# Linear attention with a gated feed-forward block in float32: plain token pairs taken from the half that stays on chip, the sum of k by accumulating transfers, and two results kept in PSUM

## The chip, the cores and the metric

The kernel runs on one core of a Trainium2 chip. The metric is the time of one execution in device microseconds; lower is better. PE is TensorE (PEld its weight loads), DVE is VectorE, ACT is ScalarE, POOL is GpSimd, and SP is SyncE, which issues nearly all transfers.

## The reference

With x of 2048 tokens by 512, everything in float32:

```
xn  = layernorm(x)
q, k, v = split(xn @ wqkv)                    # 32 heads of 16
phi(t) = where(t > 0, t + 1, exp(t)) + 1e-6
kv  = sum over tokens of phi(k)^T v           # per head
z   = sum over tokens of phi(k)
s   = (phi(q) @ kv) / (phi(q) . z + 1e-6) @ wo
g   = silu((gelu(xn @ w_gate) * (xn @ w_up)) @ w_down)     # w_gate, w_up: 512 x 1792
out = x + s * g
```

## The kernel before

**Products.** A float32 operand is split into a high part, a copy in a reduced type made by ACT, and a low part, the difference, made by DVE. A product is three matmuls (high-high, high-low, low-high; `sum3`, line 531 of the profile). Large products go by a seven-product scheme for blocks of two by two: seven products instead of eight, with sums of blocks (S1 to S4 of weights, T1 to T4 of tokens, the "forms") made ahead and results put together behind (X, Y, Z banks; c11, c12, c21, c22).

**Tokens.** The 16 blocks of 128 tokens are taken in eight pairs (`PAIRED`), one block from each group of four, so that a pair gives two rows of blocks. Each block is loaded (x), normalised on DVE with a power on POOL in the middle (`ln`: statistics, mv, ve, rstd on POOL, xn), and transposed (pairs 0 to 4 on PE into a PSUM bank pt, pairs 5 to 7 by DVE and transfers, `turned_in`). ACT copies pt to xt. `split_x` makes the high and low slots 0 to 2 of the transposed block, `forms` the slots 3 to 6 out of T1 to T4.

**The first two pairs** (`CL = 2`) are *plain*: their k and q are made with all eight products (`plain`: 12 matmuls for each block and each of k and q, in two halves), so that work can start before the sums of the weights are ready. Their forms are needed in the feed-forward block alone. Pairs 2 to 7 use the seven products (`first_products`, `rest`). For each block, phi of k goes to SBUF (kp, `phi` and `k_out`), is added to zacc on POOL, split to pks, and multiplied with xn into four banks (`gacc`, gps in the profile). phi of q (qp) is stored to memory by SP. kp and qp share three SBUF buffers, used in turn. wk1, wk2, wq1 and wq2 are the quarters of the weights, kq and a their split forms.

**The halves.** The slots of eight token blocks fit in SBUF at a time (`XT`, four places j). Pairs 0 to 3 are the first half, tokens 0 to 1023; `spill_x` stores their slots (xh_d, xl_d). Pairs 4 to 7 overwrite them and stay. The feed-forward block then runs over the second half, loads the first half's slots again, and runs over it in the opposite order of units. `queries`, `kv_part` and `m_part` run beside it; the products S with the result of attention and the output end the program.

**Order.** Every operation is recorded with a cost and an engine. `Plan.order` lays them on the engines in a list schedule whose priorities are the numbers of the table `PRIORITY`. The order of each engine's instructions is fixed by it; an engine runs its own in that order and waits where a result is missing. The fills and warm-up matmuls (`warm`, `filler`) are matmuls of ones, with no result used, that stand where PE would be idle.

Of the kernel before, what the change touches and what calls it, by code (L numbers as in the profile page):

```python
# [9 lines left out]
F32 = mybir.dt.float32  # L10
# [8 lines left out]
WARM = 11  # L19
WARM2 = 2  # L20
CL, TURN = 2, 5
PAIRED = [(8 * (n // 4) + n % 4, 8 * (n // 4) + 4 + n % 4) for n in range(8)]
# [1455 lines left out]
```

## Time and profile before

| | |
|---|---|
| median of 3 runs | 594.05 us (593.21 to 594.99) |
| the profiled execution | 595.51 us, span 593.7 us |
| PE busy | 583.8 us, 2602 matmul records |
| DVE, ACT, POOL busy | 486.3, 322.6, 358.7 us |
| granted clock of PE | 0.999 |
| transfers | 148.37 MB, 250 GB/s on average |

A row of the timeline gives the start, the time, the engine, the line, the operation and what it writes and reads (buffer numbers left out), then how many are merged (x8) and, in brackets, the idle time before it and what ended that. In a row of groups the total busy time and the mean of one in ns stand behind the bar, then the idle time before them. A matmul record shows the whole passage through the array, so records that follow each other overlap; the distance of their starts is what a matmul takes. The k and q projections fill about the first 135 us, the two feed-forward passes nearly all of the rest.

### The profile page before, as it was taken

The page shows a single profiled execution, that of the slowest core. Times are in us where ns is not written, and L with a number is a line of the kernel's source. Part 1 is how long each engine was busy: PE and PEld are TensorE (multiplying, and loading weights), DVE is VectorE, ACT ScalarE, POOL GpSimd, SP SyncE. Part 2 cuts the span into 40 slices and gives each one's busy share as a digit, 9 for nine tenths or more (in the row PEclk, how much of TensorE's full clock was granted, in tenths as well). Part 3 has the DMA queues.
Part 4 walks back from the last instruction along what each step waited for, and adds up shares of the span by engine and source line. Part 5 has one row for each costly group of instructions (what it writes and reads, how often), then busy time and mean ns, then how long its engine had stood idle before and what let it go on. Part 6 is the DMA issues. An engine that isn't in the chain of part 4 may idle for free.

```text
span 593.7 us, 8103 instructions
## 1 busy us (share of the span) xinstructions
PE 583.8 (98%) x2602; PEld 480.2 (81%) x2602; DVE 486.3 (82%) x719; ACT 322.6 (54%) x588; POOL 358.7 (60%) x301
## 2 busy tenths in 40 slices
PE   8999999999999999999999999999999999999995
PEld 8888878887888888888888878888788888887884
DVE  6989999784898987988998975677457887779996
ACT  6867768866676654575454225534325530456841
POOL 4735475425896966877678425266334562656886
PEclk9999999999999999999999999999999999999999
DMA  8378644546958756974659999779759986899536
GB/s 288 111 230 292 192 110 125 142 160 231 353 202 283 245 211 213 335 266 160 213 189 374 354 324 343 232 277 298 266 201 323 409 288 217 272 339 361 183 116 266
DMA packets 80969, 148.37 MB, mean 250 GB/s; under 512 B 18592, under 2 KB 34208, under 8 KB 80928
## 3 DMA queue, kind: packets, MB, share of 16 engines
q1 hardware_dynamic: 80928, 147.87, 72.1%
q8 instruction: 20, 0.33, 0.2%
q14 instruction: 21, 0.17, 0.1%
HBM read 83.62 MB, written 64.23 MB: 249 GB/s over the span
## 4 chain that ended last, share of the span: by engine, by line
PE 84%; DMA 6%; DVE 5%; ACT 1%; POOL 1%; issue 1%; SPq 1%; DVEq 0%; ACTq 0%; POOLq 0%
PE FX L531 24%; PE FZ L531 12%; PE DX L531 12%; PE FY L531 6%; PE DZ L531 5%; PE gps L531 5%; PE X L531 4%; PE SX L531 3%; PE DY L531 3%; PE k L531 2%; PE q L531 2%; PE Z L531 2%; PE SZ L531 2%; DMA w<-w_d 1%; DMA pn_d<-wide 1%; DMA wide<-g_d 1%
## 5 line engine op out<-in xcount | busy, mean ns | idle before, releaser
L531 PE MATMUL FX<-Xh,w 128*128 128x512 f32 x448 | 152.3, 390 | 0.8 <-DMA w<-w_d 0.6
L1078 POOL TENSOR_TENSOR h<-h,g 128x512 f32<-128x512 f32 x42 | 63.7, 1520 | 74.8 <-DVE h L515 72.6
L531 PEld LDWEIGHTS FX<-Xh,w 128*128 128x128 f32 x448 | 83.9, 188 | 19.4 <-ACT g L1070 1.0
L515 POOL TENSOR_TENSOR h<-h,h 128x512 f32<-128x512 f32 x56 | 83.2, 1486 | 18.8 <-DVE hf3l L515 6.7
L531 PE MATMUL FX<-Xl,w 128*128 128x512 f32 x224 | 87.3, 390 | 0.0
L531 PE MATMUL FZ<-Xh,w 128*128 128x512 f32 x224 | 77.7, 389 | 0.0
L509 ACT COPY fu<-FX 128x512 f32<-128x512 f32 x56 | 32.9, 587 | 58.3 <-PE FX L531 39.7
L531 PE MATMUL gps<-pks,xns 128*128 128x512 f32 x192 | 51.1, 391 | 0.0
L531 PEld LDWEIGHTS FZ<-Xh,w 128*128 128x128 f32 x224 | 42.1, 188 | 8.7
L531 PEld LDWEIGHTS FX<-Xl,w 128*128 128x128 f32 x224 | 42.1, 188 | 8.7
L515 POOL TENSOR_TENSOR wide<-wide 128x256 f32<-128x256 f32 (+1 forms) x38 | 38.9, 1035 | 15.2 <-DVE m L515 5.5
L800 POOL TENSOR_TENSOR zacc<-zacc,kp 128x512 f32<-128x512 f32 x16 | 25.9, 1617 | 36.7 <-DVE kp L789 36.4
L1104 DVE TENSOR_TENSOR acc<-acc,DX 128x512 f32<-128x512 f32 x48 | 32.2, 680 | 14.4 <-PE DX L531 14.1
L531 PE MATMUL FZ<-Xl,w 128*128 128x512 f32 x112 | 43.6, 389 | 0.0
L531 PEld LDWEIGHTS gps<-pks,xns 128*128 128x128 f32 x192 | 35.7, 188 | 7.5 <-DVE pks L798 0.2
L531 PE MATMUL FY<-Xh,w 128*128 128x512 f32 x112 | 39.1, 390 | 0.0
L1070 ACT ACTIVATE g<-g 128x512 f32<-128x512 f32 x42 | 26.5, 633 | 20.5 <-DVE g L515 20.4
L515 POOL TENSOR_TENSOR wide<-q,zacc 128x512 f32<-128x512 f32 x16 | 21.0, 1335 | 27.1 <-DMA q<-q_d 21.1
L509 ACT COPY fe<-FX 128x512 f32<-128x512 f32 x28 | 16.4, 586 | 31.8 <-PE FX L531 23.1
L531 PE MATMUL X<-kq,Xh 128*128 128x512 f32 x96 | 31.1, 391 | 0.0
L1104 DVE TENSOR_TENSOR acc<-acc,DZ 128x512 f32<-128x512 f32 x32 | 21.7, 682 | 8.6 <-PE DZ L531 8.5
L515 DVE TENSOR_TENSOR h<-fu,FZ 128x512 f32<-128x512 f32 x28 | 19.1, 682 | 11.1 <-ACT fu L509 4.5
(369 smaller groups left out, 1553.8 us busy)
## 6 DMA issues: line engine op xcount, KB each, us to landing
w_d<-w SPq DMA_DIRECT2D x36, 512.0 KB, 4.8
w<-w_d SPq DMA_DIRECT2D x36, 512.0 KB, 6.2
wd_d<-wd SPq DMA_DIRECT2D x21, 512.0 KB, 4.5
wd<-wd_d SPq DMA_DIRECT2D x21, 512.0 KB, 5.1
x<-in_first SPq DMA_DIRECT2D x16, 256.0 KB, 3.2
q_d<-qp SPq DMA_DIRECT2D x16, 256.0 KB, 2.2
q<-q_d SPq DMA_DIRECT2D x16, 256.0 KB, 5.2
pn_d<-wide SPq DMA_DIRECT2D x16, 256.0 KB, 5.4
```

The source lines that it names most:

```text
L509: do("ACT", act(n), lambda o, i: nc.scalar.copy(o, i), dst, src, name=name)
L515: do(eng, c, lambda o, p, q: getattr(e, f"tensor_{op}")(o, p, q), dst, a, b, name=name)
L531: nc.tensor.matmul(o, v[i], v[i + 1], start=start and part == 0 and i == 0, stop=stop and part == 1 and i == len(v) - 2, skip_group_check=on)
L800: do("POOL", pool(D), lambda o, i: nc.gpsimd.tensor_add(o, o, i), zacc, p0, name="zacc")
L1070: curved("gelu", do("ACT", curve(NC), lambda o, i: nc.scalar.activation(o, i, AF.Gelu_apprx_tanh), g, ps if e is None else g, name="gelu"))
L1078: do("POOL", pool(NC), lambda o, i: nc.gpsimd.tensor_mul(o, o, i), h, g, name="h")
L1104: do("DVE", dve(NC), lambda o, i: nc.vector.tensor_add(o, o, i), a, ps, name="acc")
```

## The change

- `SEQ` takes the pairs in another order: the two plain pairs are now the first two of the half that stays, then come the four of the half that leaves, then the last two that stay. `LOC` and `XTS` give their places; `spill_x` goes by `SEQ[n] < 4`.
- The forms of the two plain pairs are made behind those of pairs 5 and 6 (`FORMS`).
- zacc is summed by accumulating transfers, issued by POOL (`gather`), in place of 16 additions on POOL.
- c11 and c12 are written over the PSUM bank that they come from (`IN_PLACE`).
- For pairs 2, 3 and 4 (`FROM_PT`), T1, T2 and T3 are made by DVE out of the bank pt, T4 stays on POOL, and ACT copies half of the second block's pt.
- The transposes without a bank of their own use bank 2, that of Y, in place of bank 1.
- One low part of wk2 moves from POOL to DVE. The warm-up has 9 + 2 matmuls in place of 11 + 2, the fills are 3, 2 and 1 in place of 4, 5 and 2.
- The first two blocks are normalised side by side, and the table of numbers that sets the order is another one throughout.

```diff
-WARM = 11
+WARM = 9
+FORMS = {5: 0, 6: 1}
+IN_PLACE = ("c11", "c12")
+FROM_PT = (2, 3, 4)
+PT_BANK = 2
+SEQ = [4, 5, 0, 1, 2, 3, 6, 7]
-PAIRED = [(8 * (n // 4) + n % 4, 8 * (n // 4) + 4 + n % 4) for n in range(8)]
+PAIRED = [(8 * (n // 4) + n % 4, 8 * (n // 4) + 4 + n % 4) for n in SEQ]
+XTS = [3, 4, 5, 12, 13, 5, 3, 5]
+LOC = [0, 1, 2, 3, 2, 3, 2, 3]
 ...
 PRIORITY = """
-702 946 1004 2779 932 2336 513 1054 ...
 ...
+    def gather(dst, src, name):
+        op = do("POOL", 1.0, lambda o, i: nc.gpsimd.dma_start(o, i, accum_op=ALU.add), dst, src, name=name)
+        op.port, op.land = False, 2.5
 ...
-        kq_split(1, wk2, k, eng="POOL")
+        kq_split(1, wk2, k, eng="POOL" if k in (1,) else "DVE")
 ...
-        pt = early.get((n, i)) or bank(1, f"pt{t}", (P, KT, P))
+        pt = early.get((n, i)) or bank(PT_BANK, f"pt{t}", (P, KT, P))
 ...
-        copy("ACT", xts[n, i], pt, D, f"xt{n}{i}")
+        if i and n in FROM_PT:
+            copy("ACT", xts[n, i][:, 0:2], pt[:, 0:2], 2 * P, f"xt{n}{i}")
+        else:
+            copy("ACT", xts[n, i], pt, D, f"xt{n}{i}")
 ...
+    def part_of(n, i, k):
+        if n in FROM_PT and i:
+            return pts[n, 1][:, 2 * k:2 * k + 2]
+        return xts[n, i][:, 2 * k:2 * k + 2]
 ...
-        tt("POOL", "sub", s(0), b[:, 0:2], a[:, 0:2], 256, "T1")
-        tt("POOL", "sub", s(1), b[:, 2:4], s(0), 256, "T2")
-        tt("POOL", "sub", s(2), b[:, 2:4], b[:, 0:2], 256, "T3")
-        tt("POOL", "sub", s(3), a[:, 2:4], s(1), 256, "T4")
+        eng = "DVE" if n in FROM_PT else "POOL"
+        tt(eng, "sub", s(0), b[0], a[0], 256, "T1")
+        tt(eng, "sub", s(1), b[1], s(0), 256, "T2")
+        tt(eng, "sub", s(2), b[1], xts[n, 1][:, 0:2] if n in FROM_PT else b[0], 256, "T3")
+        tt("POOL", "sub", s(3), a[1], s(1), 256, "T4")
 ...
-        c = U(*places, name)
+        c = ps if name.split("_")[0] in IN_PLACE else U(*places, name)
         tt("DVE", "add", c, e, ps, D, name)
 ...
-        do("POOL", pool(D), lambda o, i: nc.gpsimd.tensor_add(o, o, i), zacc, p0, name="zacc")
+        gather(zacc, p0, "zacc")
 ...
-                filler(("T", 0, 0), 4)
-        forms(n)
+                filler(("T", 0, 0), 3)
         if n >= CL:
+            forms(n)
 ...
-                        filler(("K", 0, 0, 0), 5)
-                        filler(("T", 0, 1), 2)
+                        filler(("K", 0, 0, 0), 2)
+                        filler(("T", 0, 1), 1)
 ...
-        if n < 4:
+        if SEQ[n] < 4:
             spill_x(n)
+        if n in FORMS:
+            forms(FORMS[n])
```

The order moves at the very start. On PE, before, from the warm-up to the end of the first block's k projection (pt are transposes, k_267 the projection, kq the weights, Xh and Xl the parts of the tokens, b those of the second block):

```order
L553 MATMUL warm<-ones 128x128 x11
L553 MATMUL warm_232<-ones 128x128 x2
L729 MATMUL pt_241<-ident,xn_230 128x128 x4
L553 MATMUL fill_248<-ones 128x128 x4
L531 MATMUL k_267<-kq_225,Xh_259 128x512 x3
L531 MATMUL k_267<-kq_225,Xl_265 128x512
L531 MATMUL k_267<-kq_225,Xh_259 128x512
L531 MATMUL k_267<-kq_225,Xl_265 128x512
L531 MATMUL k_267<-kq_225,Xh_259 128x512 x2
L553 MATMUL fill_293<-ones 128x128 x3
```

and now, where k_272 is the first block's projection and k_295 the second's:

```order
L596 MATMUL warm_186<-ones 128x128 x2
L596 MATMUL warm<-ones 128x128 x9
L781 MATMUL pt_249<-ident,xn_240 128x128 x4
L781 MATMUL pt_256<-ident,xn_242 128x128 x4
L596 MATMUL fill_264<-ones 128x128 x2
L574 MATMUL k_272<-kq_234,Xh_262 128x512 x2
L596 MATMUL fill_264<-ones 128x128
L574 MATMUL k_272<-kq_234,Xh_262 128x512
L574 MATMUL k_272<-kq_234,Xl_277 128x512
L574 MATMUL k_272<-kq_234,Xh_262 128x512
L574 MATMUL k_272<-kq_234,Xl_277 128x512
L574 MATMUL k_295<-kq_234,b_0_283 128x512 x2
```

The second block's transpose now stands ahead of the first projection, and products of the second block stand between the halves of the first.

On DVE, now, the piece that ends with the low part Xl_361 of the second block, which the second k projection waits for (ahead of it stand the first two xn, two kq, two statistics and two Xl):

```order
L718 BN_AGGR mv_299<-st_291 128x2
L718 BN_AGGR mv_299<-st_267 128x2
L720 TENSOR_SCALAR ve_304<-mv_299 128x2
L554 TENSOR_TENSOR kq_234<-wide,kq_234 128x512
L554 TENSOR_TENSOR b_0_283<-pt_256,b_0_283 128x256
L735 TENSOR_SCALAR xn_325<-x_209,mv_299,rstd_314 128x512
L735 TENSOR_SCALAR xn_329<-x_216,mv_299,rstd_314 128x512
L554 TENSOR_TENSOR a_337<-wide,a_306 128x512
L554 TENSOR_TENSOR kq_327<-wq_223,kq_319 128x512
L554 TENSOR_TENSOR xns_289<-xn_242,xns_289 128x512
L554 TENSOR_TENSOR Xl_361<-pt_256,Xh_293 128x256
```

A kq that POOL made, the a and kq of the q weights, and the xn of the second pair now stand ahead of that Xl.

On POOL, before, the first additions to zacc among the forms T of the plain pairs:

```order
L515 TENSOR_TENSOR T_335<-xt_253,T_335 128x256
L800 TENSOR_TENSOR zacc<-zacc,kp_367 128x512
L515 TENSOR_TENSOR T_335<-xt_253,T_335 128x256
L515 TENSOR_TENSOR T_402<-xt_371 128x256
L800 TENSOR_TENSOR zacc<-zacc,kp_408 128x512
L679 TENSOR_TENSOR rstd_444<-ve_435,neg_half 128x2
```

and now, the first of the accumulating transfers, up to the first T4 of pair 2:

```order
L722 TENSOR_TENSOR rstd_314<-ve_304,neg_half 128x2
L557 DMA zacc<-kp_385 128x512
L557 DMA zacc<-kp_398 128x512
L722 TENSOR_TENSOR rstd_471<-ve_466,neg_half 128x2
L557 DMA zacc<-kp_423 128x512
L557 DMA zacc<-kp_495 128x512
L722 TENSOR_TENSOR rstd_573<-ve_567,neg_half 128x2
L554 TENSOR_TENSOR T_638<-xt_600,T_638 128x256
```

The forms of the plain pairs are gone from here, and each transfer but the first waits on POOL for the landing of the one ahead of it.

More of the change, by code (lines that the diff above doesn't have):

```diff
@@ L18 @@
 EPS = 1e-6
-WARM = 11
+WARM = 9
 WARM2 = 2
 CL, TURN = 2, 5
-PAIRED = [(8 * (n // 4) + n % 4, 8 * (n // 4) + 4 + n % 4) for n in range(8)]
+FORMS = {5: 0, 6: 1}
+ON_ACT = ()
+IN_PLACE = ("c11", "c12")
[5 more added lines that the diff above has]
+LOC = [0, 1, 2, 3, 2, 3, 2, 3]
 XS = [t for pair in PAIRED for t in pair]
@@ L223, in do @@
         op.kb = kb / self.RATE + gap if kb else 0.0
+        if not kb:
+            op.land = 0.0
         op.port = eng == "POOL" or eng == "DVE" and cost > 0.25 and not any(v.psum for v in views)
@@ L260, in hop @@
     def hop(self, p, s):
+        if p.eng == "POOL" and p.land:
+            return p.land
         if p.eng == "SP":
@@ L553, in warm @@
             nc.tensor.matmul(o, w, w, start=True, stop=True)
-    do("PE", 4.7, warm, bank(0, "warm", (P, P)), ones, key="warm")
+    do("PE", 3.84, warm, bank(0, "warm", (P, P)), ones, key="warm")
     do("PE", 0.43 * WARM2, lambda o, w: warm(o, w, WARM2), bank(7, "warm2", (P, P)), ones, key="warm2")
@@ L680, in ln @@
            rstd, ve, neg_half)
+        by_act = XS.index(ts[0]) // 2 in ON_ACT
+        if by_act:
+            shift = little("sh", f"shift{ts[0]}", [P, n])
+            do("DVE", 0.075, lambda o, m, r: nc.vector.scalar_tensor_tensor(o, m, -1.0, r, op0=ALU.mult, op1=ALU.mult),
+               shift, mv[:, :, 0], rstd, name="shift").port = True
         for i, t in enumerate(ts):
             xns[t] = U("xn", range(4, 9), f"xn{t}")
+            if by_act:
+                do("ACT", curve(D), lambda o, i, r, b: nc.scalar.activation(o, i, AF.Identity, bias=b, scale=r),
+                   xns[t], xs.pop(t), rstd[:, i:i + 1], shift[:, i:i + 1], name=f"xn{t}")
+                continue
             do("DVE", 0.456, lambda o, i, m, r: nc.vector.tensor_scalar(o, i, m, r, op0=ALU.subtract, op1=ALU.mult),
@@ L686 @@
     xts, Ts, pts = {}, {}, {}
-    early = {(0, 1): bank(4, "pt4", (P, KT, P)), (1, 0): bank(5, "pt1", (P, KT, P)), (1, 1): bank(6, "pt5", (P, KT, P))}
+    early = {(0, 1): bank(4, "pt4", (P, KT, P)), **{(1, i): bank(5 + i, f"pt1{i}", (P, KT, P)) for i in range(2) if CL > 1}}
     def filler(after, n):
@@ L718, in transp @@
         if i == 0:
-            xts[n] = D2(3 + n % 3, f"xt{n}").map(lambda ap: ap.rearrange("p a (k c) -> p a k c", c=P))
+            xts[n] = D2(XTS[n], f"xt{n}").map(lambda ap: ap.rearrange("p a (k c) -> p a k c", c=P))
         v = xts[n]
@@ L730, in transp @@
         do("PE", 0.52, run, pt, xns[t], ident, key=("T", n, i), name="T")
-        copy("ACT", xts[n, i], pt, D, f"xt{n}{i}")
+        if i and n in FROM_PT:
+            copy("ACT", xts[n, i][:, 0:2], pt[:, 0:2], 2 * P, f"xt{n}{i}")
+        else:
+            copy("ACT", xts[n, i], pt, D, f"xt{n}{i}")
         pts[n, i] = pt
+    def part_of(n, i, k):
+        if n in FROM_PT and i:
+            return pts[n, 1][:, 2 * k:2 * k + 2]
+        return xts[n, i][:, 2 * k:2 * k + 2]
     def forms(n):
-        a, b = xts[n, 0], xts[n, 1]
+        a, b = [[part_of(n, i, k) for k in range(2)] for i in range(2)]
         T = Ts[n] = D2(ring("T", [1, 2]), f"T{n}").map(lambda ap: ap.rearrange("p a (s k c) -> p (a s) k c", s=2, c=P))
@@ L746, in forms @@
                 lambda ap: ap.rearrange("p s k c -> p (s k) c"))
-            split(xblock("h", 3 + 2 * i, 5 + 2 * i, n % 4), xblock("l", 3 + 2 * i, 5 + 2 * i, n % 4), by_slot(src), D, f"XT{i}")
+            split(xblock("h", 3 + 2 * i, 5 + 2 * i, LOC[n]), xblock("l", 3 + 2 * i, 5 + 2 * i, LOC[n]), by_slot(src), D, f"XT{i}")
     def split_x(n, i):
@@ L753, in split_x @@
         elif i == 0:
-            split(xblock("h", 0, 2, n % 4), xblock("l", 0, 2, n % 4), by_slot(pts.get((n, 0), xts[n, 0])), D, "Xa")
+            split(xblock("h", 0, 2, LOC[n]), xblock("l", 0, 2, LOC[n]), by_slot(pts.get((n, 0), xts[n, 0])), D, "Xa")
         else:
-            split(xblock("h", 2, 3, n % 4), xblock("l", 2, 3, n % 4), by_slot(pts.get((n, 1), xts[n, 1])[:, 2:4]), 2 * P, "Xb")
+            split(xblock("h", 2, 3, LOC[n]), xblock("l", 2, 3, LOC[n]), by_slot(pts.get((n, 1), xts[n, 1])[:, 2:4]), 2 * P, "Xb")
     def prod(ps, n, i, start):
         ws, xsl = PRODUCTS[i]
-        xv = [xslot(hl, xsl, n % 4) for hl in "hl"]
+        xv = [xslot(hl, xsl, LOC[n]) for hl in "hl"]
         sum3(("A", n, i), ps, [((xv[0][:, k], xv[1][:, k]), (kq(ws, 0, k), kq(ws, 1, k))) for k in range(2)],
@@ L822, in spill_x @@
         for hl in "hl":
-            a, b = [xblock(hl, *XCUT[i], n).map(lambda ap: ap.bitcast(F32)) for i in range(2)]
-            do("SP", 0.475, move_both, x_d[hl](n, (slice(None), slice(None), n)), a, b, kb=896, kind="pieces", name="pieces")
+            a, b = [xblock(hl, *XCUT[i], LOC[n]).map(lambda ap: ap.bitcast(F32)) for i in range(2)]
+            do("SP", 0.475, move_both, x_d[hl](SEQ[n], (slice(None), slice(None), SEQ[n])), a, b, kb=896, kind="pieces", name="pieces")
     def first_products(n):
@@ L841, in plain @@
         ps = bank(ring("plain", [0, 2, 3]), f"{'q' if is_q else 'k'}{n}{i}")
-        xv = [[xslot(hl, s, n % 4) for hl in "hl"] for s in range(3)]
+        xv = [[xslot(hl, s, LOC[n]) for hl in "hl"] for s in range(3)]
         if i == 0:
```

267 rows, old and new, of the table PRIORITY are left out of this document.

## The prediction

> **What bounds the kernel now.** I read the page's busy times first, then its chain, then TensorE's own waits.
>
> ```profile
> PE 583.8 (98%) x2602; PEld 480.2 (81%) x2602; DVE 486.3 (82%) x719; ACT 322.6 (54%) x588; POOL 358.7 (60%) x301
> ...
> PE 84%; DMA 6%; DVE 5%; ACT 1%; POOL 1%; issue 1%; SPq 1%; DVEq 0%; ACTq 0%; POOLq 0%
> ```
> ```profile
> PE warm L553 <- DVE neg_half L544: 1.1, 1, 1.1
> PE k L531 <- ACT Xh L509: 0.6, 1, 0.6
> PE FX L531 <- DMA w<-w_d: 0.6, 1, 0.6
> PE DX L531 <- DVE acc L1104: 0.5, 1, 0.5
> PE pkv L1236 <- DMA wide<-g_d: 0.5, 1, 0.5
> PE FX L531 <- DVE w L515: 0.2, 1, 0.2
> PE Y L531 <- ACT Xh L509: 0.2, 1, 0.2
> ```
> PE is the bound, and its named waits come to 3.7 us in all, 1.8 of them in the feed-forward stage (0.6 + 0.5 + 0.5 + 0.2). The change takes no product away, so freeing POOL or ACT gains nothing by itself. Only three kinds of PE time can go: waits, fills, and a slow start. So the next view is the timeline of the first 25 us, the engines together and then PE alone.
>
> ```profile
> 1.12 5.41 PE L553 MATMUL warm<-ones 128*128 128x128 f32 x26 [1.12 <-DVE neg_half L544]
> 5.15 0.55 DVE L683 TENSOR_SCALAR xn<-x,mv,rstd 128x512 f32<-128x512 f32 x1 [0.68 <-POOL rstd L679]
> 5.21 1.14 ACT L509 CAST kq<-wk 128x512 fp32r<-128x512 f32 x2 [3.13 <-DMA wk<-in_first]
> 6.36 0.60 PE L729 MATMUL pt<-ident,xn 128*128 128x128 f32 x4
> 6.80 1.06 PE L553 MATMUL fill<-ones 128*128 128x128 f32 x8
> 7.30 0.57 ACT L509 COPY xt<-pt 128x512 f32<-128x512 f32 x1
> 7.77 0.64 ACT L509 CAST Xh<-pt 128x256 fp32r<-128x256 f32 x2
> 8.47 0.97 PE L531 MATMUL k<-kq,Xh 128*128 128x512 f32 x3 [0.61 <-ACT Xh L509]
> 9.91 1.31 ACT L509 CAST a<-wide 128x512 fp32r<-128x512 f32 x2 [0.97 <-DMA wide<-in_first]
> 12.46 1.38 PE L553 MATMUL fill<-ones 128*128 128x128 f32 x8
> ...
> 17.09 0.39 PE L531 MATMUL k<-kq,Xl 128*128 128x512 f32 x1
> 17.31 0.84 PE L531 MATMUL k<-kq,Xh 128*128 128x512 f32 x3
> ...
> 23.43 1.52 PE L531 MATMUL gps<-pks,xns 128*128 128x512 f32 x6
> 24.79 0.84 PE L531 MATMUL k<-kq,Xh 128*128 128x512 f32 x3
> ```
> The last two rows give the price of a product: 1.36 us for six, 0.227 each. From the first transpose (6.36) to the end of the two k projections of the first pair (17.31) PE took 10.95 us. It had 24 products (5.45) and four transposes of at most 0.44 (6.36 to 6.80) to do, 7.2 in all. So 3.7 us are fills and waits. This is the largest loss of PE time anywhere, and the change rewrites just this place.
>
> **The start, worked out.** I follow the new order with the durations of these rows of DVE:
>
> ```profile
> 5.86 1.29 DVE L515 TENSOR_TENSOR kq<-wk,kq 128x512 fp32r<-128x512 f32 x2 [0.17 <-ACT kq L509]
> 7.27 0.70 DVE L674 BATCH_NORM_STATS2 st<-x 128x6 f32<-128x512 f32 x1
> 8.45 0.42 DVE L515 TENSOR_TENSOR Xl<-pt,Xh 128x256 fp32r<-128x256 f32 x1 [0.27 <-ACT Xh L509]
> 10.37 0.24 DVE L675 BATCH_NORM_AGGREGATE mv<-st 128x2 f32<-128x6 f32 x2
> 11.04 0.68 DVE L515 TENSOR_TENSOR xns<-xn,xns 128x512 fp32r<-128x512 f32 x1
> 11.64 0.15 DVE L677 TENSOR_SCALAR ve<-mv 128x2 f32<-128x2 f32 x1
> 12.67 1.00 DVE L683 TENSOR_SCALAR xn<-x,mv,rstd 128x512 f32<-128x512 f32 x2 [0.88 <-POOL rstd L679]
> ```
> Both first tokens are now loaded ahead of wk1. One more statistics instruction (about 0.6) stands ahead of the first xn, which ends at 6.3 instead of 5.7. The warm-up is 11 instructions instead of 13. At 5.41 us for 26 passes, two to an instruction, its 22 take 4.6 and end near 5.7, so PE waits some 0.6 us for xn, but the transpose starts at 6.3 to 6.4, as before. Then ACT has the two Xh casts ahead of the xt copy: pt is ready at 7.0, the casts end at 7.7, and the first k product starts at 7.75 instead of 8.47, with the second transpose already done.
>
> What ends the stretch is DVE, which has no pause in it. From its first xn (5.7) to the Xl that closes the second k projection stand four xn (2.0), two kq (1.3), two statistics (1.4), two Xl (0.8), two mv and a ve (0.4), kq (0.7), b (0.4), a, kq and xns (2.0) and Xl (0.4): 9.4 us, so that Xl ends at 15.1. Rows that follow each other overlap a little on DVE (kq: two in 1.29, one such row alone 0.68), 0.08 a row, which takes it to 13.6 at best. Three products still need it: 14.3 to 15.8. PE's own work sets the lower end: 24 products, two transposes and four fills from 7.75 on are 14.5. ACT's queue is no later: one wk2 cast waits for the seventh load. With the third landed at 5.2 and the ninth at 9.9 (the two ACT rows with a DMA behind them), that is 0.78 apiece and 8.3; the casts end at 9.4, and the products that use them stand behind 9.5. PE reaches the point of 17.31 at 15.3, between 14.5 and 15.8: **2.0 us earlier, 1.5 to 2.8**. The five fills (ten passes) and two warm-up instructions that go are inside this figure. With the pauses that remain in the new order (the first Xl: 5.7 + 1.0 + 1.3 + 0.7 + 0.4 = 9.1; b, cast behind the wk2 casts, near 10; six fills) it agrees to 0.2.
>
> **The middle (15 to 150).** These are the groups of POOL and DVE in that stretch, and two windows:
>
> ```profile
> L800 POOL TENSOR_TENSOR zacc<-zacc,kp 128x512 f32<-128x512 f32 x16 | 25.9, 1617 | 36.7 <-DVE kp L789 36.4
> L515 POOL TENSOR_TENSOR T<-xt 128x256 f32<-128x256 f32 x14 | 15.3, 1095 | 13.3 <-ACT xt L509 9.4 <-DMA w_d<-w 3.9
> ...
> L798 DVE SCALAR_TENSOR_TENSOR pks<-kp,pks 128x512 fp32r<-128x512 f32 x16 | 14.0, 876 | 0.3
> L515 DVE TENSOR_TENSOR Xl<-T,Xh 128x512 fp32r<-128x512 f32 x16 | 13.1, 822 | 1.0 <-ACT Xh L509 1.0
> ...
> L789 DVE SCALAR_TENSOR_TENSOR kp<-c,kr 128x512 f32<-128x512 f32 x12 | 8.0, 683 | 0.5 <-issue 0.5
> ...
> 20.00:30.00 10.00, 10.00 (x45) 8.26 (x44) 9.82 (x20) 7.62 (x14) 7.13 (x6) 1.00 0.19 66
> ...
> 60.00:70.00 10.00, 10.00 (x45) 8.00 (x44) 10.00 (x17) 7.82 (x14) 6.47 (x5) 1.00 0.64 211
> ```
> DVE (third busy figure of a window, after PE and PEld) is at 9.8 to 10 of 10 us here, so its load decides whether the lead of PE lasts. Added: nine subtractions of 128x256 out of PSUM (0.42 each, 3.8) and one kq (0.7). Moved behind 100 us: four low halves of the plain pairs' forms (0.82 each, 3.3). Shortened: pks and Xl take 876 and 822 ns, where kp, of the same size, takes 683. They are longer beside POOL, and POOL loses the 25.9 us of zacc and nine of its T rows. The excess is 16 x 0.19 + 16 x 0.14 = 5.3 us, of which about half should go. The sum is 4.5 - 3.3 - 2.6 = -1.4 us for DVE: the lead is not eaten.
>
> c11 and c12 in PSUM add no instruction, but hold Y's and Z's banks until kp has read them, and the transposes now share Y's bank. The tightest place is the Y of the fourth pair: 13 products (2.95 us) stand between the transpose that fills its bank and Y. The bank needs 0.6 + 0.4 + 0.4 + four DVE rows of 0.42, partly side by side: 2.4 to 3.1. So 0 to 0.2 us there, and at most 0.5 for each of three such pairs; a gain of the 0.2 of the Y wait is as likely. I take 0, with -0.3 and +1.5.
>
> **The gathers.** No row shows an accumulating transfer. Each waits on POOL for the one before it to land, and holds its kp buffer that long; there are three such buffers, used in turn by kp and qp.
>
> ```profile
> q_d<-qp SPq DMA_DIRECT2D x16, 256.0 KB, 2.2
> ...
> g_d<-acc SPq DMA_DIRECT2D x8, 256.0 KB, 6.7
> ```
> ```profile
> L800 POOL TENSOR_TENSOR zacc<-zacc,kp x16: 1283/1620/2886, 15.9 to 134.5; 128x512 f32<-128x512 f32 x16
> ```
> The bounds of its landing time L are the first two rows: the same source and size, and the slowest move of that size. I take 3.0, near the first, as transfers take only 0.19 of the 16 engines from 20 to 30 us. The first two gathers stand back to back, and qp of the first token overwrites the second one's buffer. The kp of both lie 1.4 us apart on DVE, and 14 rows stand between the second kp and that qp: seven of whole blocks (0.68), two statistics (0.70), b and Xl (0.42), two mv and a ve, 7.4 us. So it is late by 2L - 8.8 us: nothing up to L = 4.4, and 4.6 us at L = 6.7. Behind it on DVE stand the two xn of the next transposes and the last plain kp, so PE would stop for nearly all of it. Later uses lie 9 us and more apart and wait only beyond L = 6. I take 0, with 0 and +4.6. On POOL itself the rstd behind a gather needs a ve that comes 5 us later, so it is free.
>
> "SBUF — State Buffer" of the Trainium skill (SBUF: two separate sides) speaks against this: a transfer issued by GpSimd cannot get its descriptors written while VectorE holds the shared port, and 620 ns alone became 3100 ns in its measurement. An estimate by that page adds 2.5 us to L, so 5.5, and would make the sum 2.2 us worse. The rows of pks and Xl above agree that the two engines block each other here; no row shows it for a descriptor.
>
> **The rest.** Spills of the leaving half come later on SP, and the x loads that stood behind them come earlier. FFN keeps its products; the last 59 rows of PE, and DVE's last 20, are the same, so the tail stays. The 1.8 us of waits there are at places whose DMA and DVE neighbours are slightly reordered: 0, between -1.0 and +1.0.
>
> **Sum.** -2.0 + 0 + 0 + 0 against the profiled 595.5 gives 593.5; the median shown is 1.5 lower, so I expect 594.05 - 2.0 = **592.0**.
>
> **Rivals.** (1) *The start's lead is not there*, since DVE's queue fills up with what used to stand behind it (s, kq and a splits of wq1 and wq2), and the first gps and q products wait for pks and a. For it: DVE's 9.8 of 10 us from 20 on. Against: the lows moved out. Only the 0.7 of the earlier first product stays: 593.3. (2) *The gather is slow*, from L = 4.4, and turns the sign from 2L - 8.8 = 2.0, so L = 5.4; it is slower by more than 0.3% from L = 6.3, and at g_d's 6.7 ends at 592.0 + 4.6 = 596.6. How it can come without slow transfers: zacc as an instruction took 1.28 to 2.89 us (the row behind them), so up to 1.6 of it was waiting for DVE; one such wait makes L 4.6 (592.4), two make it 6.2 (595.6). For it: the port rows, the chain of 16. Against: q_d's 2.2. (3) *The clock comes later.* The warm passes take 0.208 each, the fills behind them 1.06 / 8 = 0.13, so PE is about 1.6 times slower at first. The shorter warm-up and the gap behind it could leave the first projection in that state: 12 x 0.227 x 0.6 = 1.6 more, half of it inside the waits at 9.1 and 10, so 592.8. Against: the switch lies inside 5.4 us of the old warm-up. "TensorE: Matmul & The Clock Gate" of the Trainium skill (Part 1) says that full speed is granted after a busy window of about 3.4 us that does not start with the kernel. By that rule it can fall behind the gap; the trace agrees as far as the one switch goes. (4) *POOL's relief reaches PE*: with 35 us of POOL rows gone, pks and Xl shrink to 683 throughout, the Y wait goes, the weight forms of the first units (POOL, then DVE) come earlier, and FFN's waits fall by 1.0 to 1.3: 592.0 - 1.5 = 590.5. Against: two of the three larger FFN waits are on DMA.
>
> **How the numbers follow.** My forecast 0.44, (4) 0.12, (1) 0.15, (3) 0.07, (2) 0.22. A measurement of this kernel tells about 0.3% (1.8 us) from no change, so faster is below 592.3. The forecast itself falls on that edge: with its bounds three fifths of it are faster (0.26), with all of (4) and 0.05 from the better ends of (1) and (3). Of (2) 0.07 ends about level (the one or two waits for DVE), and 0.05 of slower comes from banks and FFN at their worst together. That gives faster 0.43, same 0.37, slower 0.20. The range reaches from (4) with the start's best to L near 6.4: 589.8 to 596.0; the likeliest case alone spans 591.2 to 592.5.
>
> **What would show it.** Right: first k product near 7.8, the sixth k group (now 17.31) near 15.3, PE dense from there, gathers landing within 4.4 us, and qp of the first token with no wait on a transfer. Wrong: DVE rows qp or kp waiting on zacc's transfer (2); pt or Y waiting on DVE kp (banks); products 0.36 apart after 6.3 (3); or the lead there at 17 us and gone at 60 (1).

## The result, and the profile after

The changed kernel takes 601.84 us (median of 6 runs, 598.87 to 604.70) against 594.15 us before (6 runs): ratio 1.0128, 95% interval 1.0093 to 1.0163. It is slower by 7.7 us, where 592.0 was forecast and the range ended at 596.0. The profiled execution, the slowest of the six, took 604.7 us with a span of 602.8; before it was 595.5 and 593.7. So the two profiles lie 9.1 us apart, and it is this difference that the rows explain.

Busy times and the chain, from the page of the changed kernel:

```profile
PE 586.0 (97%) x2588; PEld 478.2 (79%) x2588; DVE 484.5 (80%) x729; ACT 322.3 (53%) x588; POOL 333.9 (55%) x291
...
PE 82%; DMA 6%; DVE 6%; ACT 2%; issue 1%; SPq 1%; POOL 1%; DVEq 0%; POOLq 0%
```

DVE lost 1.8 us, near the 1.4 forecast; POOL lost 24.8, less than the 35 of the prediction, since the 16 issues themselves take 14.4. PE is still the bound, so look at its waits (time in all, times, longest):

```profile
PE gps L574 <- ACT pks L858: 1.9, 1, 1.9
PE FX L574 <- DMA w<-w_d: 1.6, 1, 1.6
PE gps L574 <- DVE pks L859: 1.5, 3, 0.7
PE pt L781 <- DVE xn L735: 1.2, 1, 1.2
...
PE q L574 <- DVE qp L850: 1.0, 1, 1.0
PE FY L574 <- DVE g L554: 0.9, 1, 0.9
PE pt L781 <- DVE kp L850: 0.6, 1, 0.6
```

With the warm-up's 1.1, as before, and three small ones (0.4, 0.3, 0.2) these are 10.7 us; before they were 3.7. The 7.0 more are most of the 9.1. A further 1.7 is no wait at all. It shows in two windows of the changed kernel around the longest stall (third to last figure: the granted clock of PE):

```profile
110.00:112.40 2.40, 0.52 (x3) 0.10 (x1) 1.39 (x3) 0.80 (x3) 1.59 (x3) 1.00 0.81 196
112.40:116.60 4.20, 4.18 (x11) 3.32 (x12) 3.46 (x7) 3.15 (x6) 0.62 (x1) 0.59 0.79 201
```

After PE had stood still for 1.9 us the clock was at 0.59 on average for 4.2 us: eleven records of product there, where 18 fit at 0.227, so 1.7 us are lost. (By the trace it is 1.00 up to 113.2 and then 0.50 for 3.4 us.)

Where does the time go along the program? The next table is worked out from both traces: at places of the product stream with the same work still to do, it gives how much later PE is than in the kernel before (us; places by the time before).

```
place, us              20    30    60    80   100   110   160   300   end
changed kernel       -0.9   0.5   0.5   2.4   3.1   7.1   7.9   7.7   9.2
```

The start is 0.9 ahead; all of that and 7.9 us more are lost between 20 and 160, that is in the projections, and nearly half of it at one place, 100 to 110 (112 to 117 in the changed kernel's own time).

**The transfers.** Issues of the changed kernel (size each, median us from issue to landing), and what DVE and POOL wait for:

```profile
zacc<-kp POOLq DMA_DIRECT2D x16, 256.0 KB, 3.9
q_d<-qp SPq DMA_DIRECT2D x16, 256.0 KB, 2.6
```
```profile
DVE qp L850 <- DMA zacc<-kp: 4.1, 2, 2.1
DVE kp L850 <- DMA zacc<-kp: 1.1, 1, 1.1
```
```profile
POOL zacc L557 <- DMA zacc<-kp: 11.4, 4, 4.7
```

A landing takes 3.3 to 5.5 us by the trace, 3.9 in the middle, so the 3.0 of the prediction was low but its threshold of 4.4 looked safe. Still DVE stands three times. The first is the qp that the prediction named, on DVE and, for the two transfers ahead of it, on POOL:

```profile
27.65 0.69 DVE L850 SCALAR_TENSOR_TENSOR qp<-q,qr 128x512 f32<-128x512 f32 x1 [2.03 <-DMA zacc<-kp]
```
```profile
18.19 1.05 POOL L557 DMA_DIRECT2D zacc<-kp  x1 [6.01 <-DVE kp L850]
24.23 0.87 POOL L557 DMA_DIRECT2D zacc<-kp  x1 [5.00 <-DVE mv L718]
```

The first transfer lands at 23.69, the second is issued 0.54 later and lands at 27.55; then DVE goes on. (The row names DVE's mv, which ended at 24.0. With four buffers, below, the landing alone ends this wait, and the step is 0.55.) Why did the first take 5.5 us? These are the DMA queues (packets, MB, share of the 16 engines) from 18 to 21.9 us, then from 21.9 to 24:

```profile
q0 software_dynamic: 135, 0.25, 36.4%
q8 instruction: 1, 0.02, 2.1%
```
```profile
q0 software_dynamic: 9, 0.02, 5.5%
```

At 21.3 us 135 of its 144 packets are through, on fifteen of the 16 engines. The last nine run from 22.0 to 23.4, one behind the other, right behind the one packet of q8, a load of instructions that takes 20.7 to 22.0. (That the two share an engine is read from these times; the trace does not name it.) Without them the landing would have been near 21.6, so 3.4 us after the issue, by an estimate from the 0.27 us between last packet and landing.

The other two waits come from two transfers back to back again (issued at 100.24 and 105.78, landing at 105.38 and 110.92). The first wait is for the one landing, the second for both, now on DVE ahead of the longest stall of PE:

```profile
105.50 0.69 DVE L850 SCALAR_TENSOR_TENSOR qp<-X,qr 128x512 f32<-128x512 f32 x1 [2.10 <-DMA zacc<-kp]
...
111.01 0.69 DVE L850 SCALAR_TENSOR_TENSOR kp<-Z,kr 128x512 f32<-128x512 f32 x1 [1.06 <-DMA zacc<-kp]
```
```profile
112.42 1.88 PE L574 MATMUL gps<-pks,xns 128*128 128x512 f32 x5 [1.90 <-ACT pks L858]
```

### The profile page after: what moved, and what is told of

Read it like the earlier page. It is cut to its first block, busy times and chain, and to the rows that moved or that the text cites. A ratio compares the mean times of both kernels' runs of the same rounds, so it can differ in the third digit from the quotient of the medians.

```text
span 602.8 us, 8122 instructions
## 1 busy us (share of the span) xinstructions
PE 586.0 (97%) x2588; PEld 478.2 (79%) x2588; DVE 484.5 (80%) x729; ACT 322.3 (53%) x588; POOL 333.9 (55%) x291
## 3 DMA queue, kind: packets, MB, share of 16 engines
q1 hardware_dynamic: 80928, 147.87, 71.1%
## 4 chain that ended last, share of the span: by engine, by line
PE 82%; DMA 6%; DVE 6%; ACT 2%; issue 1%; SPq 1%; POOL 1%; DVEq 0%; POOLq 0%
PE FX L574 24%; PE DX L574 12%; PE FZ L574 12%; PE DZ L574 6%; PE FY L574 6%; PE gps L574 4%; PE X L574 3%; PE DY L574 3%; DMA zacc<-kp 2%; PE SX L574 2%; PE Z L574 2%; DMA w<-w_d 1%; PE SZ L574 1%; PE q L574 1%; PE k L574 1%
## 5 line engine op out<-in xcount | busy, mean ns | idle before, releaser
L557 POOL DMA_DIRECT2D zacc<-kp x16 | 14.4, 902 | 51.7 <-DVE kp L850 26.8
L1133 ACT ACTIVATE g<-g 128x512 f32<-128x512 f32 x42 | 26.6, 632 | 18.8 <-DVE g L554 18.7
L554 POOL TENSOR_TENSOR wide<-q,zacc 128x512 f32<-128x512 f32 x16 | 20.8, 1323 | 21.2 <-DMA q<-q_d 12.1
L554 DVE TENSOR_TENSOR g<-fu,FZ 128x512 f32<-128x512 f32 x28 | 19.1, 682 | 15.0 <-PE FZ L574 8.2
L548 ACT COPY fe<-FX 128x512 f32<-128x512 f32 x28 | 16.4, 587 | 27.1 <-PE FX L574 19.7
```

Source lines behind the costliest of these rows:

```text
L548: do("ACT", act(n), lambda o, i: nc.scalar.copy(o, i), dst, src, name=name)
L554: do(eng, c, lambda o, p, q: getattr(e, f"tensor_{op}")(o, p, q), dst, a, b, name=name)
L557: op = do("POOL", 1.0, lambda o, i: nc.gpsimd.dma_start(o, i, accum_op=ALU.add), dst, src, name=name)
L1133: curved("gelu", do("ACT", curve(NC), lambda o, i: nc.scalar.activation(o, i, AF.Gelu_apprx_tanh), g, ps if e is None else g, name="gelu"))
```

## The experiments

Theory A: the transfers hold the three buffers of kp and qp, because each waits for the landing of the one before and then for its own, and DVE stands for the buffer. Rivals: B, the PSUM banks that c11, c12 and the T sums now hold; C, the new order of the feed-forward stage. Those that came later (D to G) are told in the expectations. In every experiment the compute engines execute their instructions in the order of the kernel it is made from, so that only the edit and what it does to buffers differ.

### The transfers as POOL adds again

```diff
-        op = do("POOL", 1.0, lambda o, i: nc.gpsimd.dma_start(o, i, accum_op=ALU.add), dst, src, name=name)
+        op = do("POOL", 1.0, lambda o, i: nc.gpsimd.tensor_add(o, o, i), dst, src, name=name)
```

> The changed kernel with every instruction of every engine in its place; only the 16 accumulating transfers of kp into zacc are POOL adds again. Theory A (the transfer holds kp's buffer and the next transfer waits for the landing of the one before, so that DVE's next kp or qp is late): the PE gaps that end at 28.4 (1.1 us), 64.1 (0.8), 76.3 (0.8), 86.1 (0.6), 95.9 (0.6) and 112.4 (2.1 and about 1.9 of half-rate products behind it) go, 7.9 us together: 594 us, 593 to 596. Rival B (the held PSUM banks: c11 and c12 in place and three T sums read from PSUM): the gaps stay, 600 to 602. Rival C (the gaps are in what the FFN's new order does, 153 to 590): 600 to 602 too, but with the early gaps gone and the later ones grown.

Measured: 599.66 us, ratio 1.0095 (1.0080 to 1.0111). Between the theories. The wait at 112 us shrinks from 1.9 to 0.2 us and the clock stays up, but others come in its place, nearly all with DVE's own rows behind them, among them:

```profile
PE k L574 <- DVE b L554: 0.7, 1, 0.7
PE Y L574 <- DVE Xl L554: 0.6, 1, 0.6
...
PE Z L574 <- DVE c L554: 0.6, 1, 0.6
```

DVE is busy 112.9 of the 120 us from 20 to 140 here; with the transfers (four buffers, below) it is 104.8. The new order has no room for the adds, so this run undoes one cost and makes another.

### The transfers alone, in the kernel before

```diff
-        do("POOL", pool(D), lambda o, i: nc.gpsimd.tensor_add(o, o, i), zacc, p0, name="zacc")
+        do("POOL", pool(D), lambda o, i: nc.gpsimd.dma_start(o, i, accum_op=ALU.add), zacc, p0, name="zacc")
```

> The kernel before with every instruction in its place; only its 16 POOL adds of kp into zacc become accumulating transfers. Theory A: its three kp buffers are held the same way, gaps of 4 to 8 us between 17 and 140: 598 to 602 us. Rival B: nothing but the sum of k differs and POOL is relieved, so 593 to 595. Rival C: 593 to 595.

Measured: 596.12 us, ratio 1.0033 (1.0017 to 1.0050). Below A's 598, above B's and C's. DVE waits once for a transfer (kp at 136.65, 1.6 us), and PE does not stop for it. PE's one new wait behind the start, 1.0 us at 73, comes another way, over POOL:

```profile
70.64 0.86 POOL L800 DMA_DIRECT2D zacc<-kp  x1 [4.33 <-DMA zacc<-kp]
71.21 1.03 POOL L679 TENSOR_TENSOR rstd<-ve,neg_half 128x2 f32<-128x2 f32 x1
72.27 0.55 DVE L683 TENSOR_SCALAR xn<-x,mv,rstd 128x512 f32<-128x512 f32 x1 [2.32 <-POOL rstd L679]
```

POOL stands for the landing of the transfer before, its rstd comes behind that, DVE's xn waits for rstd, and qp, which PE waits for, comes behind xn. The prediction had called rstd free; in the changed kernel no wait of PE comes this way. In the old order the transfers cost 2 us (1.0 to 3.0 by the interval), of which these rows show 1.0; so the order decides how much the same 16 transfers cost.

### Four buffers, and two sums

```diff
-    def added(e, ps, name, places=("c", range(13, 16))):
+    def added(e, ps, name, places=("c", range(13, 15))):
...
-        p0 = U("p", range(18, 21), f"{nm}p{t}")
+        p0 = in_order("p", [18, 19, 20, 15], f"{nm}p{t}")
```

> The changed kernel, orders kept, with four buffers for kp and qp instead of three (the fourth is one that c11 and c12 no longer use), the transfers kept. Theory A: a phi needs the buffer of the fourth phi before it instead of the third, so most waits go: early gaps of at most 3 us instead of 7.9, 594 to 598. Rival B and C: as the changed kernel, 600 to 603.

```diff
+    def to_sum(o, i):
+        issued.append(1)
+        if len(issued) == 1:
+            nc.gpsimd.dma_start(zsum(), i)
+        else:
+            nc.gpsimd.dma_start((o, zsum())[len(issued) % 2], i, accum_op=ALU.add)
...
-        op = do("POOL", 1.0, lambda o, i: nc.gpsimd.dma_start(o, i, accum_op=ALU.add), dst, src, name=name)
+        op = do("POOL", 1.0, to_sum, dst, src, name=name)
```

> The changed kernel, orders kept, three buffers, but the transfers go in turn into two sums, which one POOL add joins behind the last (one instruction more on POOL). Theory A with the serial wait as the larger part: a transfer no longer waits for the landing before it (11.4 us of POOL's idle time in four waits), DVE's waits shrink to a single landing: 595 to 599. If one landing of 3.3 to 5.5 us by itself is what holds the buffer too long: 600 to 602. Rival B and C: 600 to 603.

Measured: 599.05 us, 1.0085 (1.0070 to 1.0100), and 599.03 us, 1.0086 (1.0071 to 1.0101). Both medians are 2.8 us below the changed kernel's (the intervals just overlap), and both miss most of what A gave them, the two sums at A's edge. With four buffers the waits at 27 and 105 us are gone, but a longer one stands where the third was, on DVE:

```profile
108.88 0.69 DVE L859 SCALAR_TENSOR_TENSOR kp<-Z,kr 128x512 f32<-128x512 f32 x1 [3.05 <-DMA zacc<-kp]
```

With two sums the waits at 27 and 111 are gone and the one at 105, for a single landing, stays (2.4 us). So each takes away one of the two ways, and the other still holds.

### Both together

The two edits above; the fourth buffer (unit 14) serves from the tenth phi on, which leaves one buffer to `added`.

> The changed kernel, orders kept, with two sums for the transfers and, from the tenth phi on, four buffers for kp and qp. Theory A (the transfers hold buffers, in two ways: the wait for the landing before, and the landing itself): DVE's waits on zacc's transfer go, and with them the PE gaps near 28 (1.1 us) and 110 to 112 (2.1, and the half-rate products behind it); against the kernel before, PE is then behind by 1 to 2.5 us at the place of 120 us (7.1 in the changed kernel, 5.0 with four buffers alone, 3.2 with two sums alone), and the time is 596 to 598. Rival D (what holds PE at 110 is the turned x that lands late, or DVE's load, and not kp's buffer): the gap stays at 1.4 us or more, 598.5 to 600.

Measured: 597.53 us, ratio 1.0052 (1.0032 to 1.0072). DVE's waits on zacc shrink from 5.2 us to 0.3, and 0.0076 of the 0.0128 is gone, 4.5 us: A's share. But the stall at 110 us does not go as A had it: 1.4 us of waiting stay, as rival D said. Its cause is now in the open, on ACT:

```profile
108.74 0.40 ACT L557 CAST Xh<-xt 128x256 fp32r<-128x256 f32 x1 [2.57 <-DMA xt<-xb_d]
109.05 0.58 ACT L557 COPY e<-X 128x512 f32<-128x512 f32 x1
109.52 0.63 ACT L876 ACTIVATE pks<-kp 128x512 fp32r<-128x512 f32 x1
```

kp is ready at 107.2, but pks stands on ACT behind the cast of a turned x (the seventh pair's second block) that has not come back from DRAM, and gps waits for pks. It was sent at 97.4 and is there at 108.7, 11.3 us; the kernel before takes 7.4 for the same block. Why? The DMA queues and issues (us to landing) of this kernel from 97 to 104 us, then of the kernel before from 86 to 97, where it turns the same pair:

```profile
q1 hardware_dynamic: 2038, 1.56, 70.4%
q0 software_dynamic: 191, 0.36, 29.9%
...
xl_d<-Xl SPq DMA_DIRECT2D x1, 640.0 KB, 4.2
xb_d<-xb SPq DMA_DIRECT2D x2, 256.0 KB, 4.1
...
xt<-xb_d SPq DMA_DIRECT2D x4, 64.0 KB, 6.3
```
```profile
q1 hardware_dynamic: 3529, 1.42, 46.4%
...
xb_d<-xb SPq DMA_DIRECT2D x2, 256.0 KB, 2.2
xt<-xb_d SPq DMA_DIRECT2D x8, 64.0 KB, 2.7
```

The way back (xt) takes 6.3 us instead of 2.7 from issue to landing. The 16 engines are full (70.4 + 29.9), where they were half idle. Two loads are new there. One is the transfers: q0 moves 0.36 MB in 29.9% of 7 us, 5.8 us of all engines for a MB, against 3.2 for q1 in the same row. The other is the spill (xl_d): before, the leaving pairs came first and were stored by 68 us; now the plain pairs are of the half that stays, the leaving pairs come third to sixth, and their stores stand among the turned x. (The slow store that the expectations below name is the next pair's; this block loses its time on the way back.)

### c11 in SBUF, and the T sums on POOL

```diff
-IN_PLACE = ("c11", "c12")
+IN_PLACE = ("c12",)
```

> Two sums, three buffers, orders kept, and c11 again in SBUF instead of in Y's bank. Theory B1 (the bank of Y, held until kp has read it, delays the transposes that share it): the gap of PE behind which pt waits for kp near 63 us (0.8 us) goes, 0.8 less than with two sums alone (599.0): 598.2, 597.5 to 598.7. Rival E (DVE's queue is late there whatever holds the bank): a gap of 0.5 us or more stays within 5 us of that place, 598.7 to 599.5.

```diff
-FROM_PT = (2, 3, 4)
+FROM_PT = ()
```

> Two sums, four buffers, orders kept, and all T sums from SBUF on POOL again: nine rows of 0.42 us leave DVE, nine of about 0.73 come to POOL. Theory E (DVE's load between 40 and 95 us is what makes pks late, gps <- DVE pks 0.8, 0.7 and 0.4 us with four buffers): these three gaps go or halve, 1 to 2 us less than with both sums and buffers: 594.5 to 596. Rival F (T on POOL comes later, and POOL's rows slow DVE's by the port): the same or more than with both, 597 to 599.

> Two sums, three buffers, c11 in SBUF and all T sums on POOL, orders kept. If B1 and E both hold: the bank gap (0.8) and half or more of the pks gaps (1 to 2) go against two sums alone (599.0): 596 to 597.3. If POOL's sums cost what they give (F): 598 to 599.

Measured for c11 in SBUF: 597.96 us, ratio 1.0059 (1.0036 to 1.0082), against 1.0086 (1.0071 to 1.0101) for two sums alone. The time lies in B1's band, but the trace reads as E: the wait of pt for kp is gone, and PE stops 0.4 us at the same place for X instead of 0.6. The profile with c11 in SBUF also started 0.7 us earlier, from the landing of the first loads, so the two times do not decide; the bank alone is worth 0.2 us at this place. The T sums on POOL, with ACT copying the whole of pt again, gain nothing: 599.15 us, 1.0076 (1.0049 to 1.0103), against 1.0052 with both, and, with c11 in SBUF too, 600.05, 1.0089 (1.0064 to 1.0114), against 1.0059. Both medians are higher and above F's bands, but the intervals overlap. E's guess on DVE's load, 594.5 to 596, falls, and the change's reading of T sums from PSUM on DVE is not what costs the time; that POOL's rows slow DVE's, as F has it, these times do not show.

### The load on the DMA engines

Three runs take theory D apart, on top of both sums and buffers, and one puts the load into the kernel before.

```diff
+    moved, held = [], []
...
     def move_both(o, a, b):
+        moved.append(1)
+        if len(moved) in (7, 8):
+            held.append((o, a, b))
+            return
...
+        if o.name == "table":
+            while held:
+                move_both(*held.pop(0))
```

> Two sums and four buffers, orders of the four compute engines kept; the four stores of the last leaving pair's forms (1.8 MB, from 79 to 103 us) are sent only behind the last pair, where their tiles hold another pair's forms, so that part of the output is of other data. Theory D (after the waits on zacc, what stops PE near 85 and 110 us is the turned x of the sixth and seventh pair: it comes late from DRAM, and ACT's pks stands behind its cast; the store takes 5.5 us there where it took 2.0 to 3.3 before, since the moved spill and the transfers, which need about 6.0 us of engine time per MB where others need 2.9, share the 16 engines): the turned x of the seventh pair lands 1 to 2 us earlier than 108.7, the gap at 110 falls from 1.5 to 1.0 us or less, 1 us less than with both (597.5): 596 to 597. Rival G (the rows of DVE that make it simply stand later in the new order): the gap stays at 1.3 or more, 597 to 598.

```diff
+        elif len(issued) in (10, 11):
+            nc.gpsimd.tensor_add(o, o, i)
```

> Two sums and four buffers, orders kept; only the tenth and eleventh transfer (issued near 98.5 and 99.1 us, landing up to 106.4) are POOL adds. Theory D: the store of the turned x takes 2 to 3.5 us instead of 5.5, the gap at 110 falls from 1.5 to 0.8 us or less, 596 to 597. Rival G: the gap stays at 1.3 or more, 597 to 598.

> Both of these together: the last leaving pair's four stores sent behind the last pair (with another pair's forms in them) and the tenth and eleventh transfer as POOL adds. Theory D: the turned x of the seventh pair lands within 7.5 us of DVE's transposing, as before (9.4 with both sums and buffers), and the gap at 110 is 0.4 us or less; 595.5 to 596.5. Rival G: a gap of 1.2 us or more stays, 597 to 598.

Measured: 595.79 us, ratio 1.0023 (1.0007 to 1.0040), without the last spill in its place; 596.79, 1.0030 (1.0016 to 1.0045), with the two adds; 596.89, 1.0036 (1.0020 to 1.0052), with both. In all three traces no gap is left at 110 us, where the five profiles with two sums so far have one of 1.3 to 1.4. The block that took 11.3 us from its store to its last load takes 9.7, 7.4 and 7.2. Either load alone can be taken away, and x comes in time: that shows the cause, and G falls. For this block the transfers are the larger of the two. The intervals of the times overlap, with each other and with both sums and buffers, so what the gap is worth is read from the traces; where adds stand in for transfers, a new gap of 0.5 to 0.6 us for DVE's Xl comes at 102 to 104 us and eats a part. What is left of PE's waits in the run without the last spill (0.4 and 0.3 not shown, and the warm-up):

```profile
PE gps L583 <- DVE pks L877: 1.0, 1, 1.0
PE FX L583 <- ACT fe L557: 0.6, 1, 0.6
PE pt L799 <- DVE kp L868: 0.6, 1, 0.6
...
PE gps L583 <- ACT pks L876: 0.3, 1, 0.3
```

The run with both lost 2 us near 80 us instead: there the turned x of the sixth pair landed 2.1 us later than in the run without the last spill, with the same instructions up to that place. Landing times in that crowd vary from run to run.

```diff
+        for n in (4, 5):
+            if o is more[n]:
+                for hl in "hl":
+                    a, b = [xblock(hl, *XCUT[i], n % 4).map(lambda ap: ap.bitcast(F32)) for i in range(2)]
+                    move_both(extra[hl, n](), a(), b())
```

> The kernel before, orders of the four compute engines kept, with one thing added: the forms of the fifth and sixth pair are also stored to DRAM (eight stores, 3.6 MB, to a place that nobody reads), so that stores stand beside the turned x as in the changed kernel. Theory D: the share of the 16 engines between 80 and 110 us rises from 0.25 to 0.55 to over 0.7, turned x lands later, and PE gets gaps of 0.5 to 2 us there: 594.7 to 596.5. Rival G: the order before leaves 3 us between landing and use, so PE keeps its time: 594 to 594.6. If it is the transfers' traffic alone that matters: as rival G.

Measured: 597.45 us, ratio 1.0046 (1.0032 to 1.0060), 2.7 us more, above D's range. The windows of this kernel (second to last figure: share of the DMA engines, 0.25 and 0.55 before in the first and last), ACT's rows and PE's waits:

```profile
80.00:90.00 10.00, 9.60 (x42) 7.62 (x41) 9.45 (x17) 6.37 (x12) 7.33 (x8) 1.00 0.86 239
...
100.00:110.00 10.00, 8.94 (x39) 6.91 (x39) 5.71 (x10) 5.87 (x12) 3.23 (x5) 1.00 0.88 262
```
```profile
99.24 0.62 ACT L509 CAST Xh<-xt 128x512 fp32r<-128x512 f32 x1 [2.17 <-DMA xt<-xb_d]
...
107.09 0.41 ACT L509 CAST Xh<-xt 128x256 fp32r<-128x256 f32 x1 [1.75 <-DMA xt<-xb_d]
```
```profile
PE X L531 <- ACT Xh L509: 2.4, 2, 1.3
```

Stores of forms beside the turned x, with no transfer on POOL at all, stop ACT and then PE in the kernel before too. That is D by itself, with one thing left open: the eight stores also stand ahead of loads on SP, and this run does not separate their issue from their load on the engines. The two adds above do: there SP's instructions are unchanged.

## Why the prediction was wrong

The places once more, as worked out above (us later than the kernel before):

```
place, us              20    30    60    80   100   110   160   300   end
changed kernel       -0.9   0.5   0.5   2.4   3.1   7.1   7.9   7.7   9.2
four buffers         -1.2  -1.2  -1.2   0.4   1.0   5.0   5.5   5.2   3.2
both                 -0.4  -0.4  -0.3   1.0   1.4   3.3   3.9   3.6   2.8
both, no last spill  -0.9  -0.9  -0.8   0.3   1.0   1.3   2.0   1.8   0.1
```

**The gathers: this term failed.** It was given 0, with rival (2) beginning at L = 4.4. The place and the mechanism of its first wait were right: DVE's qp on the second transfer. Three things in the sum were not. It used one L for both landings, where the trace has 5.5 and 3.3; their sum is 8.8, by the formula exactly no wait. It left out the steps between: 0.33 us from the end of kp to the issue, 0.54 from one landing to the next issue. And it gave DVE 8.8 us of work where qp was reached 7.8 after the first kp. Together 0.33 + 5.5 + 0.54 + 3.3 - 7.8 = 1.9, measured 2.03. At this place it was also bad luck: with 3.4 for the first landing, the estimate above without the load of instructions, the sum is -0.2, no wait. In the nine other profiles with the new order and transfers that load starts at 19.5 to 21.2 us, so it comes each time, but what it delays varies. The sentence that later uses "lie 9 us and more apart and wait only beyond L = 6" was the larger error. At 105 us DVE came back to the buffer of the first of two transfers 3.6 us after its kp (99.84 to 103.40), so one landing of 5.1 was too long. The second of two back to back holds its buffer for two landings, and at 5.1 us each that was too long at 111. All waits of this kind cost 4.5 us of the 7.7 (ratio 1.0128 to 1.0052; 2.1 to 6.9 by their intervals), with the fall of the clock behind the longest of them, 1.7 us in the profile, which no term of the sum had.

**What SP carries: this term was not seen.** "Spills of the leaving half come later on SP" was entered at 0, and the transfers' own load on the engines was not entered at all. What they do is make the turned x late, which then holds up everything behind it on ACT. The profile before had the warning in its windows: 0.25 to 0.55 of the engines from 80 to 110 us was room that the old order kept free. This is 1.0 to 1.7 us by the ratios (1.0052 to 1.0036, 1.0030 and 1.0023), whose intervals overlap.

**The start was right in kind, and its 2.0 was near the mean.** After the same 24 products (17.31 before) the changed kernel is at 16.39, so 0.9 ahead and not 2.0, on PE:

```profile
8.18 0.74 PE L574 MATMUL k<-kq,Xh 128*128 128x512 f32 x2
...
16.39 0.85 PE L574 MATMUL k<-kq,Xh 128*128 128x512 f32 x3
```

The first product starts at 8.18 where 7.75 was forecast, since the cast of wk waits for its load until 6.03, with one more x ahead of it; before, it began at 5.21. That landing wanders: over all profiles the first gps product starts at 20.0, 21.2 and 21.1 us with the old order and at 18.8 to 19.7, on average 19.2, with the new one in eleven. The mean lead is 1.6 us, inside the 1.5 to 2.8, but three profiles of the old order, 1.2 us apart, are few. The lead is there, and gone at 28 us.

**The middle held.** DVE's work fell by 1.8 us (forecast 1.4); pks and Xl came down to 771 and 801 ns, 2.0 us in all where 2.6 was taken. No run shows a gain from moving the T sums back to POOL. The waits at Y's bank cost 0.6 at one place, inside the bounds, and mostly not by the bank. **FFN** lost 1.3 us from 160 us on in the profile, but gained 1.1 to 2.3 in the three others of the table, so the band of one us either way was too narrow and the 0 fair. **The rivals:** (2) was the case in its kind, with another price; its bound of 596.6 assumed one late place. (1) and (4) were not it: POOL's relief never reached PE, and DVE's pks holds PE up only at 76 to 96 us (1.5 us). (3) did not come at the start, where the fills between 7.5 and 8.9 us stand 0.11 apart as in the kernel before; a lower clock came at 113 us, behind the longest stall.

What stays open: some 1.4 us of the loss remain in the best of these runs (1.0023), at the waits of its list; the sixth pair's turned x, DVE's pks and the entry to the feed-forward stage are the places, and no run separates them. None of the runs beats the kernel before.

## What to carry to other kernels

Work that leaves an engine for the DMA is not free there: look at the share of the DMA engines in the windows where it will run, and at who waits for the transfers that already run in them. When a transfer takes over an in-place sum, count two landings and the steps between for the buffer behind the second, and give it a second sum or a further buffer before trusting a threshold. When the order of the data changes, ask for every store what stands beside it now.

## What was not expected of the hardware

An accumulating transfer needs about twice the engine time of a plain one here. Over the whole changed kernel q0 has 4.20 MB in 4.2% of the span and q1 147.87 MB in 71.1%:

```profile
q1 hardware_dynamic: 80928, 147.87, 71.1%
q0 software_dynamic: 2304, 4.20, 4.2%
```

That is 6.0 us of all engines per MB against 2.9. POOL's queue is not the reason: with both sums the first of the 16 goes through the same queue without adding. By the trace its 64 packets of 4096 B took 174 ns each, where those of the 15 that add carry 2048 B and took 197: 2.7 us of all engines per MB against 6.0. The issue takes POOL 0.9 us (14.4 us for 16). The page "SBUF — State Buffer" of the Trainium skill (SBUF: two separate sides), weighed in the prediction, let L come out at 5.5, an estimate, by waiting for the port. The first landing took just that, but by chance: its packets began 1.6 us after the issue, and 2.1 of the 5.5 us came with the load of instructions. The median took 3.9. Elsewhere landings grow where the engines are full (5.5 and 7.3 us at 100%); whether a wait for descriptors is a part of that, no row separates.

The clock fell after a short pause. Two waits of 1.9 and 1.8 us at 110 us were followed by 3.4 us at 0.50, which is 0.59 (changed kernel) and 0.54 (four buffers) over the windows shown; waits of 1.3 to 1.4 us at the same place were not. The second case, four buffers:

```profile
108.00:110.30 2.30, 0.46 (x3) 0.04 (x2) 1.42 (x3) 0.70 (x2) 2.00 (x4) 1.00 1.01 301
110.30:114.00 3.70, 3.70 (x9) 2.96 (x10) 3.02 (x6) 3.12 (x6) 0.58 (x1) 0.54 0.73 155
```

"TensorE: Matmul & The Clock Gate" of the Trainium skill (Why this matters for your kernels) warns of pauses above some 3 us; here 1.8 was enough, and nearly doubled the price of the stall. A pause of 2.1 us near 9 us, in the kernel before with the transfers, was not followed by it, so the length alone does not decide. The six runs of the changed kernel agree: at a mean clock of 0.998 or 0.999 they took 598.9 and 600.2 us, at 0.995 to 0.997 601.2 to 604.7.
